# One of eight pairs of h rows by seven block products, with the work around it moved

## The chip, the cores and the metric

The kernel runs on one core of a Trainium2 chip. A core has a matrix engine (TensorE, PE in the profile), two elementwise engines (VectorE, DVE; ScalarE, ACT), a general one (GpSimd, POOL, idle here) and queues that issue DMA (SyncE, SP). Each engine works through its own list of instructions; where one needs another's result it waits on a semaphore. The metric is the device time of one execution in microseconds (us), as the median of several runs.

## The reference

Four batches of 6080 tokens with 256 channels. A channel attention gives, for each batch, a 256 x 256 matrix a, and then each token goes through a feed-forward layer with a squared relu:

```python
qn = q / (np.linalg.norm(q, axis=1, keepdims=True) + 1e-06)
kn = k / (np.linalg.norm(k, axis=1, keepdims=True) + 1e-06)
s = kn.transpose(0, 2, 1) @ qn / tau
s = s - s.max(-1, keepdims=True)
a = np.exp(s)
a /= a.sum(-1, keepdims=True) + 1e-09
x = (v @ a).reshape(B * S, D)
h = np.maximum(x @ w_in, 0.0)
out = h * h @ w_out
```

x has 24320 rows of 256, h 2048 columns. The inputs are float32 except w_in and w_out, which come as float64 and are decoded in the kernel.

## The kernel before

**What is multiplied.** v @ a @ w_in is computed as v @ W, with W = a @ w_in made once per batch (256 x 2048). Each float32 operand is split into a rounded part (hi, written by ScalarE) and the rest (lo, written by VectorE as original minus hi), and each product is three matmuls: hi by hi, hi by lo, lo by hi.

**Blocks and steps.** The tokens of a batch make 12 blocks n: ten of 512 columns and two of 480. A block has 16 steps f, one for each 128 rows of h; two steps are a pair r = f // 2, and part = f % 2. The list `steps` (lines 739 to 743) has four batches of 12 blocks of 16 steps; the first two blocks are interleaved, as W of the first batch is only being made. The loop from line 794 issues, for step i, in this order:

- `first_product` (574): six matmuls of 512 columns into one PSUM tile of the pool `ps_h` (three buffers), then a ScalarE relu into half of the pair's tile x (two buffers);
- one piece of other work (`beside`): the chunks of q and k of the next batch, its softmax and its W (`attention`, 370, and `softmax_and_W`, 402), left out at f = 2 and 3. A chunk takes four steps: at its first a ScalarE cast and a VectorE subtraction, at its third a ScalarE square and a VectorE addition, at its third and fourth six matmuls each. Work at odd steps comes at the step's end;
- at an even step, `parts_of_sums` (611) of the pair before: hi (ScalarE, 1024 columns) and lo (VectorE) of the four sums;
- at an odd step, `squares_and_sums` (598) of this pair: a ScalarE square of 1024 columns, three VectorE sums (of 512, 256 and 256 columns), hi and lo of three of the squares (768 columns);
- at an odd step, one piece of `combine` (680) of the block before, at f = 5, 7 and 9;
- `second_product` (624) of the pair two pairs back (LAG = 2).

**The second product by seven.** For 45 of the 48 blocks the output's 2 x 2 block product takes seven block products, not eight (`seven_products`, 645). Its operands are the pair's squares (slots 0 to 2), their sums (slots 3 to 6), blocks of w_out and sums of them (S1n, S2, S3, S4). `SEVEN` (640) says which of the seven are issued in the even step (three) and in the odd one (four). They accumulate over the block's eight pairs in two PSUM tiles of the pool `ps_acc` (two buffers), one for each part; with the last pair, in the next block's steps 2 and 3, ScalarE copies them out (line 676). The next block's first pair takes the same two tiles at its steps 4 and 5.

**v's parts.** `load_v` brings v of a block (one buffer), `split_v_hi` and `split_v_lo` make hi (ScalarE) and lo (VectorE) of it in the block before, at f = 6 and 8 (line 831).

**Order.** ScalarE, VectorE and TensorE are wrapped in `InProgramOrder` (19): each engine's list has the order in which the Python code issues the instructions. Tiles that share a tag share its buffers; an instruction that writes a buffer waits for the last readers.

Of the kernel before, what the change touches and what calls it, by code (L numbers as in the profile page):

```python
# [30 lines left out]
def kernel(  # L31
# [25 lines left out]
    P = 128  # L57
# [5 lines left out]
    GRP = 512  # L63
    NG = F // GRP
    FPG = GRP // P
    J = 2
    NPAIR = NF // 2
    PPG = FPG // 2
# [162 lines left out]


    W = {}
    now = {"part": 0}
    HEAD = 5
    QK_BUFS = 2
    FAST_TAGS = ("qk",) * QK_BUFS + ("w_lo",) * NG + ("w_hi",) * NG

    class Gram:
# [66 lines left out]
    def start_first(b=0):  # L306

        g = grams[0] = Gram(0)
        total = g.n + HEAD
        AHEAD = len(FAST_TAGS) - 1  # L310

        room = pool.tile([P, HEAD - 1, 2, J, C], F32, tag="wS_lo", name="qk_heads", bufs=1)

        def load(c):
            if c == g.n:
                grams[1] = Gram(1)
            if c < g.n:
                g.load(c, FAST_TAGS[c % len(FAST_TAGS)])
            elif c < total and B > 1:
                grams[1].load(c - g.n, raw=room[:, c - g.n] if c - g.n < HEAD - 1 else None)  # L320

        for c in range(AHEAD):
            load(c)
        for c in range(g.n):
            if c < g.n - LAST:
                for _ in g.products(c, [(g.raws[c], g.raws[c])]):
                    pass
            g.squares(c)
            if c:
                g.add_squares(c - 1)  # L330
            load(c + AHEAD)
            if c in (2, 15):
                weights.load(int(c > 2))
            if c in (13, 14, 15, 17):
                weights.stage(0)
            if c == 19:
                load_v(*order[0])
        for c in range(g.n + AHEAD, total):
            load(c)
        g.add_squares(g.n - 1)  # L340

        def rest():
            for c in range(g.n - LAST, g.n):
                for _ in g.products(c, [(g.raws[c], g.raws[c])]):
                    pass
            yield

        return rest()
# [53 lines left out]
    def softmax_and_W(b):  # L402
# [74 lines left out]
        eT_hi = pool.tile([P, NC, C], F32R, tag="eT_hi", name=f"eT_hi{b}", bufs=1)  # L477
        eT_lo = pool.tile([P, NC, C], F32R, tag="eT_lo", name=f"eT_lo{b}", bufs=1)
# [5 lines left out]
        for g in range(NG):  # L484
            while (b, g) not in may_write_W:
                yield
            if b == 0:
                while g not in wi_first:
                    yield
                hi, lo = wi_first.pop(g)  # L490
                keep_w_in(g, (hi, lo))
            else:
                hi, lo = wi.pop(g)
            w_hi = wpool.tile([P, NC, GRP], F32R, tag="w_hi", name=f"w_hi{b}_{g}")
            w_lo = wpool.tile([P, NC, GRP], F32R, tag="w_lo", name=f"w_lo{b}_{g}")
# [27 lines left out]

            if b == 0:
                for h, terms in ((0, (0, 1)), (1, (0,)), (0, (2,)), (1, (1, 2))):
                    products(h, terms)
                yield
                for h in range(NC):
                    evict(h)
            else:  # L530
                for h in range(NC):
                    products(h)
                    if h == NC - 1 and g + 1 < NG:
                        wi[g + 1] = reload_w_in(b, g + 1)
                    yield
                    evict(h)
                    yield
            W[b, g] = w_hi, w_lo
            yield

# [16 lines left out]
    def once(f, *args):  # L557
        f(*args)
        yield

    def split_v_lo(b, n):
        tn = blocks[n][1]
        raw, hi, _ = V[b, n]
        V[b, n][2] = pool.tile([P, NC, T], F32R, tag="v_lo", name=f"v_lo{b}_{n}")
        vector.tensor_sub(V[b, n][2][:, :, :tn], raw[:, :, :tn], hi[:, :, :tn].bitcast(F32))

    def by_seven(b, n):

# [2 lines left out]
    X = {}  # L571
    G = {}

    def first_product(b, n, f):
        tn = blocks[n][1]
        _, v_hi, v_lo = V[b, n]
        w_hi, w_lo = W[b, f // FPG]
# [20 lines left out]
    def squares_and_sums(b, n, r):  # L598

        x = X[b, n, r]  # L600
        G[b, n, r] = hi, lo = parts_of(b, n, r)
        scalar.activation(x[:, 0:4, :], x[:, 0:4, :], AF.Square)
# [27 lines left out]
    def weights_of(r):  # L630
# [49 lines left out]
    def combine(b, n):  # L680
# [5 lines left out]
        vector.tensor_add(o[:, 1:3, :], o[:, 1:3, :], both(0))  # L686
        yield
        vector.tensor_add(o[:, 4, :], o[:, 4, :], o[:, 2, :])
        vector.tensor_add(o[:, 0, :], o[:, 4, :], o[:, 3, :])
        yield  # L690
        vector.tensor_add(o[:, 3, :], o[:, 3, :], o[:, 2, :])
        vector.tensor_add(o[:, 5:7, :], o[:, 5:7, :], o[:, 3:5, :])
        at = b * N + t0
        out = outT[:, at : at + tn].rearrange("(m p) t -> p m t", p=P)
        for m, k, slot in ((0, 0, 5), (0, 1, 1), (1, 0, 0), (1, 1, 6)):
            nc.sync.dma_start(out[:, m, k * half : (k + 1) * half], o[:, slot, :])
        yield

# [94 lines left out]
    beside = attention_of_others()  # L793
    for i in range(len(steps) + 2 * LAG):
        part = now["part"] = i % 2
        if i < len(steps):
            b, n, f = steps[i]
            at = b * NB + n
# [24 lines left out]
        if part == 1 and i // 2 < len(pairs):  # L823
            squares_and_sums(*pairs[i // 2])
        if part and late_work:
            if next(late_work[0], "end") == "end":
                late_work.pop(0)
        if i >= 2 * LAG:
            second_product(*pairs[i // 2 - LAG], part)
        if i < len(steps):  # L830
            at_hi, at_lo = (None, None) if at == 0 else (12, 13) if at == 1 else (6, 8)
            if i == 2 and len(order) > 2:
                load_v(*order[2])
            if f == at_hi and at + 1 < len(order):
                split_v_hi(*order[at + 1])
            if f == at_lo and at + 1 < len(order):
                split_v_lo(*order[at + 1])
                if at + 2 < len(order):
                    load_v(*order[at + 2])
        if i >= PAIR and part:  # L840
            for gen in gens:
                next(gen, None)
# [27 lines left out]
```

## Time and profile before

| | |
|---|---|
| median of 3 runs | 2220.44 us (2219.77 to 2220.57) |
| the profiled execution | 2222.8 us, of which the span from first to last instruction 2221.0 us |
| mean granted TensorE clock | 0.999 |
| matmul instructions | 13740 |
| matmuls of h (ps_h from v and w) | 3 groups of 1536, of 512 or 480 columns |
| matmuls with sums of w_out (ps_o with wS) | 3 groups of 1440, of 256 or 240 columns |

Busy times are those of an engine, its share is of the span. A group is named by output and inputs: `ps_h<-v_hi,w_hi` are matmuls that write a tile ps_h from v_hi and w_hi. All instructions show line 27, that of the wrapper, so groups are told apart by their tiles: `x<-ps_h` is the relu, `x<-x` on ScalarE the square, `x<-x` on VectorE the three sums, `g_hi<-x` the hi parts (768 columns at odd steps, 1024 at even ones), `g_lo` the lo parts, `o<-ps_o` the copy out of PSUM. A row of the timeline gives start, duration, engine, line, operation, tiles and shape, a count when several are merged, and in brackets how long the engine was idle before and for whom. The end of a matmul is modelled; the start of the next one is what counts for the pace. A row of the waits gives total us, times and the longest. A row of the windows gives the stretch, its length, busy us and instructions of PE, PEld, DVE, ACT and POOL, the granted clock, and DMA.

### The profile page before, as it was taken

How to read it: one execution, taken by the hardware profiler on the slowest of the kernel's cores; microseconds unless marked ns; L12 is line 12 of the kernel's file. 1: busy time of each engine (PE TensorE's matmuls, PEld its weight loads, DVE VectorE, ACT ScalarE, POOL GpSimd, SP SyncE). 2: the span in 40 equal slices, each digit the busy share in tenths (PEclk: the TensorE clock that was granted, in tenths of full speed). 3: DMA queues.
4: the chain of work that ended last, by engine and by line, in shares of the span. 5: the costliest groups of instructions: out<-in, count | busy, mean ns of one | idle time of the engine just before them, and what ended most of it. 6: DMA issues, size and time to landing. Idle time of an engine off the chain costs nothing.

```text
span 2221.0 us, 34359 instructions
## 1 busy us (share of the span) xinstructions
PE 2207.5 (99%) x13740; PEld 1981.4 (89%) x13740; DVE 1761.4 (79%) x2470; ACT 1844.6 (83%) x2294; POOL 0.7 (0%) x6
## 2 busy tenths in 40 slices
PE   8999999999999999999999999999999999999999
PEld 7788999989989999988998999999899888888898
DVE  6878888878778888878777888887877777787773
ACT  5788888888778888888878888888887888888885
POOL 0000000000000000000000000000000000000000
PEclk9999999999999999999999999999999999999999
DMA  9511222100211112110111122110102010010000
GB/s 334 184 67 39 69 66 67 46 29 26 70 66 58 60 60 72 62 41 22 36 68 56 60 66 75 58 53 22 33 25 76 21 36 20 22 37 20 22 26 18
DMA packets 76495, 126.99 MB, mean 57 GB/s; under 512 B 7728, under 2 KB 35120, under 8 KB 76336
## 3 DMA queue, kind: packets, MB, share of 16 engines
q1 hardware_dynamic: 76336, 124.81, 17.2%
q8 instruction: 107, 1.75, 0.3%
q14 instruction: 52, 0.43, 0.1%
HBM read 95.68 MB, written 29.10 MB: 56 GB/s over the span
## 4 chain that ended last, share of the span: by engine, by line
PE 94%; DVE 3%; ACT 1%; DMA 1%; issue 0%; SPq 0%; DVEq 0%; ACTq 0%
PE ps_h L27 46%; PE ps_o L27 41%; PE gram L27 5%; PE ps_w L27 2%; DVE g_lo L27 1%; DMA qk<-in_k 1%; DVE x L27 1%; DVE acc L27 0%; ACT x L27 0%; DMA qk<-in_q 0%; ACT g_hi L27 0%; DVE o L27 0%; PE ps_n L27 0%; ACT sq L27 0%; ACT s L27 0%
## 5 line engine op out<-in xcount | busy, mean ns | idle before, releaser
L27 DVE TENSOR_TENSOR g_lo<-x,g_hi 128x768 fp32r<-128x768 f32 (+2 forms) x744 | 804.4, 1081 | 95.2 <-ACT g_hi L27 94.5
L27 DVE TENSOR_TENSOR x<-x 128x256 f32<-128x256 f32 (+3 forms) x1080 | 551.2, 510 | 279.6 <-ACT x L27 254.7
L27 ACT CAST g_hi<-x 128x768 fp32r<-128x768 f32 (+2 forms) x744 | 697.7, 938 | 24.6 <-DVE x L27 12.0
L27 ACT ACTIVATE x<-ps_h 128x512 f32<-128x512 f32 (+1 forms) x768 | 456.1, 594 | 293.3 <-PE ps_h L27 267.7
L27 PE MATMUL ps_h<-v_hi,w_hi 128*128 128x512 f32 (+1 forms) x1536 | 478.9, 393 | 0.0
L27 PE MATMUL ps_h<-v_hi,w_lo 128*128 128x512 f32 (+1 forms) x1536 | 477.9, 392 | 0.0
L27 PE MATMUL ps_h<-v_lo,w_hi 128*128 128x512 f32 (+1 forms) x1536 | 474.9, 390 | 0.0
L27 ACT ACTIVATE x<-x 128x1024 f32<-128x1024 f32 (+1 forms) x384 | 404.5, 1053 | 11.9
L27 PE MATMUL ps_o<-g_lo,wS_hi 128*128 128x256 f32 (+1 forms) x1440 | 402.5, 279 | 1.3 <-DVE g_lo L27 1.1
L27 PE MATMUL ps_o<-g_hi,wS_lo 128*128 128x256 f32 (+1 forms) x1440 | 401.7, 279 | 0.0
L27 PE MATMUL ps_o<-g_hi,wS_hi 128*128 128x256 f32 (+1 forms) x1440 | 400.8, 278 | 0.0
L27 PEld LDWEIGHTS ps_h<-v_lo,w_hi 128*128 128x128 f32 x1536 | 288.1, 188 | 64.8
L27 PEld LDWEIGHTS ps_h<-v_hi,w_lo 128*128 128x128 f32 x1536 | 288.7, 188 | 61.8
L27 PE MATMUL ps_o<-g_hi,wo_hi 128*128 128x256 f32 (+3 forms) x1176 | 330.9, 288 | 0.9 <-ACT g_hi L27 0.9
L27 PE MATMUL ps_o<-g_hi,wo_lo 128*128 128x256 f32 (+3 forms) x1176 | 331.1, 288 | 0.0
L27 PE MATMUL ps_o<-g_lo,wo_hi 128*128 128x256 f32 (+3 forms) x1176 | 330.6, 288 | 0.1
L27 PEld LDWEIGHTS ps_o<-g_lo,wS_hi 128*128 128x128 f32 x1440 | 271.2, 188 | 18.0 <-DVE g_lo L27 2.3
L27 PEld LDWEIGHTS ps_o<-g_hi,wS_hi 128*128 128x128 f32 x1440 | 270.6, 188 | 15.4
L27 PEld LDWEIGHTS ps_o<-g_hi,wS_lo 128*128 128x128 f32 x1440 | 270.9, 188 | 0.0
L27 PEld LDWEIGHTS ps_h<-v_hi,w_hi 128*128 128x128 f32 x1536 | 239.1, 188 | 5.2
L27 PEld LDWEIGHTS ps_o<-g_hi,wo_hi 128*128 128x128 f32 x1176 | 221.7, 189 | 17.5 <-ACT g_hi L27 1.3
L27 PEld LDWEIGHTS ps_o<-g_lo,wo_hi 128*128 128x128 f32 x1176 | 221.0, 188 | 16.7 <-DVE g_lo L27 0.5
(87 smaller groups left out, 1671.4 us busy)
## 6 DMA issues: line engine op xcount, KB each, us to landing
qk<-in_k SPq DMA_DIRECT2D x87, 256.0 KB, 2.8
qk<-in_q SPq DMA_DIRECT2D x87, 256.0 KB, 3.0
v<-in_vT SPq DMA_DIRECT2D x40, 512.0 KB, 3.8
out_T<-o SPq DMA_DIRECT2D x152, 128.0 KB, 1.7
wi_hi<-wi_kept SPq DMA_DIRECT2D x12, 512.0 KB, 3.2
wi_lo<-wi_kept SPq DMA_DIRECT2D x12, 512.0 KB, 4.1
w_raw<-in_w_in SPq DMA_DIRECT2D x4, 1024.0 KB, 6.0
w_raw<-in_w_out SPq DMA_DIRECT2D x4, 1024.0 KB, 5.5
```

The lines of the kernel that those rows point to most:

```text
L27: return lambda *args, **kwargs: self.tc.keep_in_program_order(issue(*args, **kwargs))
```

## The change

It has five parts.

1. In blocks n >= 3 of the first batch and n >= 1 of the others (42 blocks), the pair r = 5 (f = 10 and 11) takes seven block products for its h. At f = 10 four of them, 12 matmuls of 256 columns into two ps_h tiles; then a chain: ScalarE copies two of them out, VectorE adds one sum (U2), adds it to both halves of the second tile in PSUM, and makes one of the four results. At f = 11 the other three products, 9 matmuls, accumulate onto what stands in PSUM, and three ScalarE relus follow.
2. For that, sums of W's blocks are made once per batch (`sums_of_W`), and sums of v's blocks once per block: `sums_of_v` at the end of f = 0 (three VectorE operations, a ScalarE cast), `sums_of_v_lo` at f = 3 (one VectorE operation).
3. At f = 10 no work goes beside, and the sums of the preceding pair, r = 4, that stood at f = 9, are issued behind the chain; at f = 11 the second product is issued ahead of the first.
4. In the second product the four products of sums are all in the odd step; `combine` uses the new slots.
5. v's hi and lo parts move from f = 6 and 8 to f = 9 and 12, v's load to f = 0. Tiles of w_in, e and one chunk of q and k share other tags.

```diff
     def wi_tiles(b, g):
-        hi = pool.tile([P, NC, GRP], F32R, tag="wi_hi", name=f"wi_hi{b}_{g}", bufs=1)
-        lo = pool.tile([P, NC, GRP], F32R, tag="wi_lo", name=f"wi_lo{b}_{g}", bufs=1)
-        return hi, lo
+        return [
+            pool.tile([P, NC, GRP], F32R, tag="qk", name=f"{name}{b}_{g}", bufs=QK_BUFS) for name in ("wi_hi", "wi_lo")
+        ]
...
+    def sums_of_W(b, r):
+        while now["dec"]:
+            yield
...
+        vector.tensor_add(w, hi, lo)
+        vector.tensor_add(S1, A21, A22)
+        vector.tensor_sub(S3, A11, A21)
+        vector.tensor_sub(S2, S1, A11)
+        vector.tensor_sub(S4, A12, S2)
...
+        scalar.copy(WS[b, r][0], S)
+        vector.tensor_sub(WS[b, r][1], S, WS[b, r][0].bitcast(F32))
...
+    def sums_of_v(b, n):
...
+        vector.tensor_sub(S[:, 0:3:2, :], raw[:, :, half:tn], raw[:, 0, :tn].rearrange("p (k t) -> p k t", k=2))
+        vector.tensor_sub(S[:, 1, :], B22, S[:, 0, :])
+        vector.tensor_sub(S[:, 3, :], B21, S[:, 1, :])
+        scalar.copy(VS[b, n][0], S)
+        now["dec"] = True
+
+    def sums_of_v_lo(b, n):
+        hi, lo, S = VS[b, n]
+        vector.tensor_sub(lo, S, hi.bitcast(F32))
...
+    def seven_first_products(b, n, r, part):
...
+        if part == 0:
...
+            product(one[:, 0], "A11", "B11", start=True)
+            product(one[:, 1], "S2", "T2", stop=True)
+            product(two[:, 0], "S1", "T1", start=True)
+            product(two[:, 1], "S3", "T3")
+            P1, P5, U2 = (x[:, i, :] for i in (4, 5, 6))
+            scalar.copy(P1, one[:, 0])
+            scalar.copy(P5, two[:, 0])
+            vector.tensor_add(U2, one[:, 1], P1)
+            vector.tensor_add(two, two, x[:, 6:7, :].broadcast_to([P, 2, half]))
+            vector.tensor_add(x[:, 3, :], two[:, 1], P5)
+        else:
...
+            product(one[:, 0], "A12", "B21", stop=True)
+            product(two[:, 0], "S4", "B22")
+            product(two[:, 1], "A22", "T4", stop=True)
+            scalar.activation(x[:, 3, :], x[:, 3, :], AF.Relu)
+            scalar.activation(x[:, 0, :], one[:, 0], AF.Relu)
+            scalar.activation(x[:, 1:3, :], two, AF.Relu)
...
     SEVEN = (
-        (None, ("A11", 0), ("A12", 2), ("S2", 5)),
-        (("S1n", 3), ("S3", 4), ("S4", 1), ("A22", 6)),
+        (None, ("A11", 0), ("A12", 2), ("S4", 1)),
+        (("S2", 5), ("S1n", 3), ("S3", 4), ("A22", 6)),
     )
...
         part = now["part"] = i % 2
+        chained, chain_next = (j < len(steps) and first_by_seven(*steps[j]) for j in (i, i + 1))
+        if chained and part:
+            second_product(*pairs[i // 2 - LAG], part)
...
-        if i >= PAIR and steps[min(i, len(steps) - 1)][2] in (2 * LAG - 2, 2 * LAG - 1):
+        if i >= PAIR and (chained and part == 0 or steps[min(i, len(steps) - 1)][2] in (2 * LAG - 2, 2 * LAG - 1)):
             gens = ()
...
+        if chained and part == 0:
+            sums_and_parts(*pairs[i // 2 - 1])
         if part == 0 and 0 <= i // 2 - 1 < len(pairs):
             parts_of_sums(*pairs[i // 2 - 1])
...
-            squares_and_sums(*pairs[i // 2])
+            squares(*pairs[i // 2])
+            if not chain_next:
+                sums_and_parts(*pairs[i // 2])
...
-        if i >= 2 * LAG:
+        if i >= 2 * LAG and not (chained and part):
             second_product(*pairs[i // 2 - LAG], part)
         if i < len(steps):
-            at_hi, at_lo = (None, None) if at == 0 else (12, 13) if at == 1 else (6, 8)
+            at_hi, at_lo = (None, None) if at == 0 else (12, 13) if at == 1 else (9, 12)
...
+            if at > FIRST - 1:
+                if f == 0 and has_sums(b, n):
+                    sums_of_v(b, n)
+                if f == 0 and at + 1 < len(order):
+                    load_v(*order[at + 1])
+                if f == 3 and has_sums(b, n):
+                    sums_of_v_lo(b, n)
```

`squares` and `sums_and_parts` are the two halves of `squares_and_sums`.

More of the change, by code (lines that the diff above doesn't have):

```diff
@@ L65 @@
     FPG = GRP // P
+    QK_BUFS = 2
     J = 2
@@ L233 @@
     W = {}
-    now = {"part": 0}
+    now = {"part": 0, "dec": False}
     HEAD = 5
-    QK_BUFS = 2
     FAST_TAGS = ("qk",) * QK_BUFS + ("w_lo",) * NG + ("w_hi",) * NG
@@ L319, in load @@
             elif c < total and B > 1:
-                grams[1].load(c - g.n, raw=room[:, c - g.n] if c - g.n < HEAD - 1 else None)
+                last = pool.tile([P, 2, J, C], F32, tag="vS_lo", name="qk_head", bufs=1) if c == total - 1 else None
+                grams[1].load(c - g.n, raw=room[:, c - g.n] if last is None else last)
         for c in range(AHEAD):
@@ L476, in softmax_and_W @@
         yield from pause(b, 2, 1)
[L477 to L478 removed]
+        eT = pool.tile([P, 2, NC, C], F32R, tag="qk_hi" if b else "vS_hi", name=f"eT{b}", bufs=1)
+        eT_hi, eT_lo = eT[:, 0], eT[:, 1]
         ps_tv = ps_t.rearrange("p (d c) -> p d c", d=NC)
@@ L572, with first_by_seven, has_sums, product @@
     G = {}
+    H = {}
+    def first_by_seven(b, n, f):
+        return has_sums(b, n) and f // 2 in SEVEN_FIRST
+    def has_sums(b, n):
+        return n >= (1 if b else FIRST)
+    def seven_first_products(b, n, r, part):
+        half = blocks[n][1] // 2
+        _, v_hi, v_lo = V[b, n]
+        def product(ps, a, b_, start=False, stop=False):
+            A, B_ = W_of[a], v_of[b_]
+            for i, (wt, vt) in enumerate(((A[0], B_[0]), (A[0], B_[1]), (A[1], B_[0]))):
+                tensor.matmul(ps, wt, vt, start=start and i == 0, stop=stop and i == 2, skip_group_check=True)
+        A = blocks_of_W(b, r)
+        W_of = {f"A{i + 1}{j + 1}": [a[i][j] for a in A] for i in range(2) for j in range(2)}
+        W_of.update({f"S{i + 1}": [p[:, i, :] for p in WS[b, r]] for i in range(4)})
+        v_of = {
+            f"B{j + 1}{k + 1}": [v[:, j, k * half : (k + 1) * half] for v in (v_hi, v_lo)] for j in range(2) for k in range(2)
+        }
+        v_of.update({f"T{i + 1}": [p[:, i, :] for p in VS[b, n][:2]] for i in range(4)})
+        if part == 0:
+            x = X[b, n, r] = pool.tile([P, 8, half], F32, tag="x", name=f"x{b}_{n}_{r}")
+            one, two = H[b, n, r] = [
+                ps_h.tile([P, 2, T // 2], F32, tag="h", name=f"ps_h{b}_{n}_{r}_{i}")[:, :, :half] for i in range(2)
+            ]
+            product(one[:, 0], "A11", "B11", start=True)
[9 more added lines that the diff above has]
+        else:
+            one, two = H.pop((b, n, r))
+            x = X[b, n, r]
+            product(one[:, 0], "A12", "B21", stop=True)
[4 more added lines that the diff above has]
+            scalar.activation(x[:, 1:3, :], two, AF.Relu)
@@ L837 @@
                 split_v_lo(*order[at + 1])
-                if at + 2 < len(order):
+                if at == 1 and at + 2 < len(order):
                     load_v(*order[at + 2])
+            if at > FIRST - 1:
[5 more added lines that the diff above has]
+                    sums_of_v_lo(b, n)
+            if i in (26, 28):
+                next(first, None)
         if i >= PAIR and part:
```

48 lines of the change are left out of this document (37 added, 11 removed).

## The prediction

> **What bounds the kernel now.** I read the page first, then the waits, then the timeline of one block engine by engine.
>
> ```profile
> span 2221.0 us, 34359 instructions
> PE 2207.5 (99%) x13740; PEld 1981.4 (89%) x13740; DVE 1761.4 (79%) x2470; ACT 1844.6 (83%) x2294; POOL 0.7 (0%) x6
> PE 94%; DVE 3%; ACT 1%; DMA 1%; issue 0%; SPq 0%; DVEq 0%; ACTq 0%
> ```
>
> The chain that ended last is TensorE for 94%. The waits say the same: ScalarE waits for TensorE, VectorE for ScalarE, and TensorE for almost nobody.
>
> ```profile
> ACT x L27 <- PE ps_h L27: 267.7, 465, 4.2
> DVE x L27 <- ACT x L27: 254.7, 276, 2.6
> PE ps_o L27 <- DVE g_lo L27: 1.1, 2, 0.7
> ```
>
> So the time is the number of matmul columns, as long as the other two engines keep their distance. How large that distance is, is read from one block without q and k work beside it (times of TensorE, from the timeline):
>
> ```profile
> 1930.13:1971.99 41.86, 41.86 (x266) 37.60 (x265) 32.26 (x47) 35.31 (x43) 0.00 (x0) 1.00 0.09 26
> 1973.20 0.63 PE L27 MATMUL ps_h<-v_hi,w_hi 128*128 128x512 f32 x2
> ...
> 1974.59 0.28 PE L27 MATMUL ps_o<-g_hi,wo_hi 128*128 128x256 f32 x1
> ...
> 1975.64 0.62 PE L27 MATMUL ps_h<-v_hi,w_hi 128*128 128x512 f32 x2
> ...
> 1977.03 0.28 PE L27 MATMUL ps_o<-g_hi,wS_hi 128*128 128x256 f32 x1
> ...
> 1978.43 0.63 PE L27 MATMUL ps_h<-v_hi,w_hi 128*128 128x512 f32 x2
> ```
>
> A block is 41.86 us and TensorE is busy in all of it. These are its steps f = 4 and 5: six 512-column products of h take 1.39 us (1973.20 to 1974.59), nine 256-column products of the output 1.05 us, twelve of them 1.40 us (1977.03 to 1978.43). Half the columns take half the time, each with its own weight load. The part of ScalarE from f = 0 to f = 4, with the last pair (7) of the block before in flight:
>
> ```profile
> 1964.32 0.60 ACT L27 ACTIVATE x<-ps_h 128x512 f32<-128x512 f32 x1 [0.23 <-PE ps_h L27]
> 1964.90 1.05 ACT L27 CAST g_hi<-x 128x1024 fp32r<-128x1024 f32 x1
> 1966.76 0.60 ACT L27 ACTIVATE x<-ps_h 128x512 f32<-128x512 f32 x1 [0.81 <-PE ps_h L27]
> 1967.39 1.06 ACT L27 ACTIVATE x<-x 128x1024 f32<-128x1024 f32 x1
> 1968.49 0.83 ACT L27 CAST g_hi<-x 128x768 fp32r<-128x768 f32 x1
> 1969.56 0.60 ACT L27 ACTIVATE x<-ps_h 128x512 f32<-128x512 f32 x1 [0.23 <-PE ps_h L27]
> 1970.13 1.05 ACT L27 CAST g_hi<-x 128x1024 fp32r<-128x1024 f32 x1
> 1971.09 0.79 ACT L27 COPY o<-ps_o 128x768 f32<-128x768 f32 x1
> 1972.00 0.60 ACT L27 ACTIVATE x<-ps_h 128x512 f32<-128x512 f32 x1
> 1972.63 1.06 ACT L27 ACTIVATE x<-x 128x1024 f32<-128x1024 f32 x1
> 1973.72 0.83 ACT L27 CAST g_hi<-x 128x768 fp32r<-128x768 f32 x1
> 1974.46 1.01 ACT L27 COPY o<-ps_o 128x1024 f32<-128x1024 f32 x1
> 1975.37 0.60 ACT L27 ACTIVATE x<-ps_h 128x512 f32<-128x512 f32 x1
> ```
>
> Two things are to be seen. The two copies of the old block's sums out of PSUM stand at f = 2 and f = 3, and the new block's products take the same PSUM at f = 4 and f = 5. The second copy ends at 1974.46 + 1.01 = 1975.47 and TensorE wants that PSUM at 1977.03: **1.56 us of slack**. And between the relu of f = 1 (1966.76) and that copy ScalarE idles 0.23 us only: what makes that relu late arrives at the copy almost whole. VectorE in the same stretch:
>
> ```profile
> 1963.26 1.61 DVE L27 TENSOR_TENSOR x<-x 128x512 f32<-128x512 f32 x3 [1.28 <-ACT x L27]
> 1964.78 0.95 DVE L27 TENSOR_TENSOR g_lo<-x,g_hi 128x768 fp32r<-128x768 f32 x1
> 1965.98 1.23 DVE L27 TENSOR_TENSOR g_lo<-x,g_hi 128x1024 fp32r<-128x1024 f32 x1 [0.25 <-ACT g_hi L27]
> ```
>
> Rules of thumb from these rows: an instruction starts 0.03 to 0.04 us after the one it needs; one that needs nothing new starts 0.1 us before the end of its predecessor.
>
> **The change part by part.** *Gain.* A pair's h now costs 2 x 1.39 = 2.78 us; by seven it is 12 + 9 products of 256 columns, 1.40 + 1.05 = 2.45 us. That saves 0.33 us in each of 42 blocks (9 of the first batch, 11 of the three others), 13.9 us; eight of them have 480 columns, so 13.7. The nine added weight loads are in it, since the narrow rows have one load each.
>
> *v's sums at f = 0.* Three VectorE operations of 512, 256 and 256 columns, the sizes of the group that took 1.61 us, and behind them a ScalarE cast of 1024 columns (1.05 us). Both engines keep the order of the program. VectorE has the wide g_lo of pair 7 ahead of them, which waits for ScalarE's wide cast: it ends at 1965.98 + 1.23 = 1967.21, the sums run from 1967.12 to 1968.73, the cast from 1968.77. Queued behind that cast on ScalarE is the relu of f = 1, which then starts at 1969.72 in place of 1966.76: **2.96 us late**, 2 us of it idling. On from there: square 1970.35 to 1971.41, VectorE's sums of pair 0 until 1973.05, so that the wide cast of f = 2 starts at 1973.09, first copy 1974.05, relu 1974.96, square, cast 1976.68, second copy 1977.42 to 1978.43. TensorE stood ready at 1977.03: it waits **1.4 us**, in a block in which all else is as before.
>
> *The chain at f = 10.* Time zero is TensorE's start of that step. The relu of f = 9 is at -1.20, the square at -0.57, v's cast (now at f = 9) at 0.39 to 1.43. The two copies of 256 columns out of PSUM aren't in the trace; the copies out of ps_o of 512 and 768 columns give 0.37.
>
> ```profile
> L27 ACT COPY o<-ps_o 128x512 f32<-128x512 f32 x4 | 2.1, 581 | 0.0
> L27 ACT COPY o<-ps_o 128x768 f32<-128x768 f32 x38 | 30.2, 795 | 0.0
> L27 DVE TENSOR_TENSOR x<-x 128x256 f32<-128x256 f32 x608 | 258.4, 425 | 20.9
> L27 DVE TENSOR_TENSOR x<-x 128x512 f32<-128x512 f32 x304 | 210.2, 691 | 199.0 <-ACT x L27 198.8
> L27 DVE TENSOR_TENSOR v_lo<-v,v_hi 128x1024 fp32r<-128x1024 f32 x40 | 48.8, 1219 | 0.0
> ```
>
> They run at 1.34 and 1.62, VectorE's three additions until 3.33. No row shows an addition that writes PSUM: I take 0.69 us, the row of its size, with the 0.43 of 256 columns and twice the 0.69, 1.4, as ends. TensorE needs the result after 12 + 9 + 12 + 3 products, at 4.20: covered by 0.87 us, so the chain itself stalls nothing. But the preceding pair's sums follow it (3.25 to 4.85) and ScalarE idles until 4.89 for its wide cast, ahead of three relus and the next square. The relu of f = 12 comes at 8.91 where TensorE had it ready at 6.49: 2.4 us late. Pairs recover up to 1.24 us each (5.24 us on TensorE, 4.0 on ScalarE), but v_lo, moved to f = 12, holds VectorE 1.14 us: late by 1.8, 1.5, 1.6 and, at f = 0, still 1.2 us. With that ahead, the relu of f = 1 is 4.5 us late, the first PSUM copy ends at 29.10 (wanted at 27.30), the second at 32.69 (wanted at 29.74): TensorE waits 1.8 and 1.2 us, **3.0 us a block**. Afterwards ScalarE catches up by f = 9, so each block pays it again.
>
> *Blocks with q and k beside them.* f = 10 takes no such work now, so a block takes 3 chunks, not 3.5, and 67 chunks fill some 22 of the 42 blocks. A chunk adds two ScalarE and two VectorE operations of 1024 columns and 1.40 us of TensorE; the same walk gives 2.0 or 2.7 us by where the chunks fall, mean 2.35.
>
> *What costs nothing.* The new order of the output's seven products needs the sums one step later: it gives them 2.45 us more, no time by itself. VectorE's second half of v's sums at f = 3 stands in VectorE's idle time. Sums of W: about 3.1 us of VectorE a batch, in blocks without v's sums, hidden by VectorE's idle 9.6 us there; uncovered, at most 12 us in all. On SP's queue v's load moves to f = 0 behind VectorE's sums, with nothing due behind it until the outputs at f = 9, and is needed 22 us later. w_in's tiles share two buffers with q and k, whose last readers are done first.
>
> ```profile
> v<-in_vT SPq DMA_DIRECT2D x40, 512.0 KB, 3.8
> ```
>
> *Sum.* 20 x 3.0 + 22 x 2.35 = 111.7 us of waits. Against the profiled execution, 2222.8 us: 2222.8 - 13.7 + 111.7 = 2320.8; it stood 2.4 us above the median of the runs, so the **forecast is 2318 us**.
>
> **The rivals.** *Hidden, 2207 us.* One mechanism puts it on the faster side: v's sums need only v, loaded long before, so if VectorE ran them ahead of pair 7's g_lo, ScalarE's cast would not idle and would cost its own 0.95 us; the point that decides is whether the relu of f = 1 is less than 1.56 + 0.23 us late. Then 2220.4 - 13.7. For it: nothing in the data ties them together. Against it: in all rows both engines run in the written order.
>
> *Only the clean wait, 2266 us.* If ScalarE and VectorE recover from the chain before f = 0, 42 x 1.4 = 59 us are lost and 13.7 won. For it: the recovery of 1.24 us a pair; against it: v_lo at f = 12.
>
> *The clock drops, about 2389 us.* The trace has one place where TensorE waited and then worked thinly:
>
> ```profile
> 45.00:50.00 5.00, 3.21 (x17) 2.76 (x17) 4.55 (x15) 0.29 (x1) 0.00 (x0) 0.93 1.05 392
> 50.00:55.00 5.00, 5.00 (x17) 3.43 (x17) 2.72 (x10) 1.52 (x3) 0.00 (x0) 0.73 0.74 244
> ```
>
> With 3.21 of 5 us busy the granted clock fell to 0.93 and then 0.73 of full, which lost 5 x 0.07 + 5 x 0.27 = 1.7 us. If each block's two waits did the same, 42 x 1.7 = 71 us come on top. Against it: the two waits have 2.45 us of dense products between them. The Trainium skill, TensorE: Matmul & The Clock Gate, section "HAM oscillation — how this bites in real kernels", asks for idle gaps above some 3.4 us before the clock drops; by that rule nothing is added here, and the sum stays. Its section "A second HAM failure mode: psum-queue depth-cycling" says that frequent short idles between groups of matmuls are enough; by that one this rival comes true. The rows just shown lean to the second, since no idle there reached 3.4 us.
>
> **How the numbers follow.** Forecast, 2.0 to 3.2 us a block, 2285 to 2340: 0.47. Clean wait, 2245 to 2285: 0.15. Part hidden, 2216 to 2245: 0.06. Hidden: 0.20. Clock: 0.12. The dear end of the PSUM addition, 0.7 us a block, would make it 2347. Leaving out the clock's case, the range is 2205 to 2345. A measurement of this kernel can tell 0.2%, about 4.4 us. Faster by more: 0.20; within: 0.03; slower: 0.77.
>
> **What would show it.** In the changed profile, the waits should have TensorE's ps_o behind ScalarE's o, over 80 us in all; ScalarE's cast of v's sums should idle 2 to 3 us behind VectorE at each f = 0, with the relu after it 3 to 5 us behind its product; the addition into PSUM should be near 0.69 us and TensorE's second half of the seven products should wait for none. If ps_o does not wait for o, the forecast is wrong at the slack of 1.56 us; if it waits 1.4 us a block, only the residue of the chain is. If TensorE waits at f = 11 for VectorE, the 0.87 us was.

## The result, and the profile after

The changed kernel takes **2325.22 us** (2325.01 to 2328.94, 4 runs) against 2220.3 us before on the same chip: a ratio of 1.0475, with a 95% interval of 1.0463 to 1.0488. It is slower by 105 us. The page of the changed kernel, with its span, the engines and the chain that ended last:

```profile
span 2323.2 us, 35621 instructions
PE 2221.4 (96%) x14118; PEld 1985.4 (85%) x14118; DVE 1925.8 (83%) x2788; ACT 1873.7 (81%) x2466; POOL 0.7 (0%) x6
DVE 38%; PE 29%; ACT 27%; issue 5%; DMA 1%; SPq 0%; DVEq 0%; ACTq 0%
```

TensorE's 94% of the chain have become 29%. The chain now runs round the three engines, although TensorE is still busy 96% of the span and VectorE and ScalarE only 83 and 81%: they wait for one another. The waits of the changed kernel (engine, what it waits for, total us, times, longest) say where:

```profile
ACT g_hi L27 <- DVE x L27: 155.6, 171, 3.5
ACT vS_hi L27 <- DVE v_sums L27: 130.9, 42, 3.7
...
ACT x L27 <- PE ps_h L27: 87.8, 131, 4.2
PE ps_o L27 <- ACT o L27: 75.0, 76, 2.8
...
PE ps_h L27 <- DVE x L27: 0.7, 1, 0.7
```

ScalarE waited 267.7 us for TensorE before, and 87.8 now. In exchange it waits 42 times for VectorE's sums of v, 3.1 us each, and TensorE waits for ScalarE's copies out of PSUM. The last row is TensorE's wait for the result of the new chain: once. One block without q and k beside it, from f = 0 to f = 5, first VectorE's timeline, then ScalarE's, then TensorE's:

```profile
2055.96 1.22 DVE L27 TENSOR_TENSOR g_lo<-x,g_hi 128x1024 fp32r<-128x1024 f32 x1 [0.25 <-ACT g_hi L27]
2057.10 0.68 DVE L27 TENSOR_TENSOR v_sums<-v 128x512 f32<-128x512 f32 x1
2057.82 0.89 DVE L27 TENSOR_TENSOR v_sums<-v,v_sums 128x256 f32<-128x256 f32 x2
```

```profile
2054.88 1.05 ACT L27 CAST g_hi<-x 128x1024 fp32r<-128x1024 f32 x1 [0.31 <-DVE x L27]
2058.74 1.05 ACT L27 CAST vS_hi<-v_sums 128x1024 fp32r<-128x1024 f32 x1 [2.81 <-DVE v_sums L27]
2059.70 0.59 ACT L27 ACTIVATE x<-ps_h 128x512 f32<-128x512 f32 x1
...
2064.01 0.79 ACT L27 COPY o<-ps_o 128x768 f32<-128x768 f32 x1
...
2067.17 1.00 ACT L27 COPY o<-ps_o 128x1024 f32<-128x1024 f32 x1
```

```profile
2062.51 0.63 PE L27 MATMUL ps_h<-v_hi,w_lo 128*128 128x512 f32 x2
2064.85 0.38 PE L27 MATMUL ps_o<-g_hi,wo_hi 128*128 128x256 f32 x1 [1.71 <-ACT o L27]
2065.08 0.28 PE L27 MATMUL ps_o<-g_lo,wo_hi 128*128 128x256 f32 x1
2065.19 0.28 PE L27 MATMUL ps_o<-g_hi,wo_lo 128*128 128x256 f32 x1
...
2066.01 0.62 PE L27 MATMUL ps_h<-v_hi,w_hi 128*128 128x512 f32 x2
...
2068.23 0.39 PE L27 MATMUL ps_o<-g_hi,wS_hi 128*128 128x256 f32 x1 [0.68 <-ACT o L27]
```

VectorE does pair 7's wide g_lo first, then v's sums; ScalarE's cast stands idle 2.81 us for them, with the relu of f = 1 queued behind it. The first copy then ends at 2064.80 and TensorE, which could have started that product at 2062.97, starts at 2064.85: 1.88 us later. At f = 5 it could have gone on at 2066.01 + 1.39 = 2067.40 and starts at 2068.23, 0.83 us later.

Block lengths below are the distances between successive first copies (`COPY o<-ps_o 128x768`) on ScalarE. Without q and k beside, a block took 41.87 us before and 44.50 us now; with q and k 46.95 (mean of two that alternate) and 48.51. To compare kernels I also count **TensorE's waits**: of all pairs of successive matmuls after the first 66 us, the time from start to start beyond the pace (0.2345 us for 512 columns, 0.1185 for 256, in proportion for 480 and 240; products of one column are left out), where it is over 0.06 us. Before that was 7.9 us in all, 4.7 of it at products of ps_o; now it is 122.1 us, 100.9 of it at products of ps_o. The largest of the others is 2.5 us, near a batch's end.

### The profile page after: what moved, and what is told of

It reads as the page before. It is cut to its first block, busy times and chain, and to the rows that moved or that the text cites. A ratio compares the mean times of both kernels' runs of the same rounds, so it can differ in the third digit from the quotient of the medians.

```text
span 2323.2 us, 35621 instructions
## 1 busy us (share of the span) xinstructions
PE 2221.4 (96%) x14118; PEld 1985.4 (85%) x14118; DVE 1925.8 (83%) x2788; ACT 1873.7 (81%) x2466; POOL 0.7 (0%) x6
## 3 DMA queue, kind: packets, MB, share of 16 engines
HBM read 95.68 MB, written 29.10 MB: 54 GB/s over the span
## 4 chain that ended last, share of the span: by engine, by line
DVE 38%; PE 29%; ACT 27%; issue 5%; DMA 1%; SPq 0%; DVEq 0%; ACTq 0%
DVE x L27 16%; ACT x L27 14%; PE ps_h L27 13%; PE ps_o L27 12%; DVE g_lo L27 10%; ACT g_hi L27 6%; DVE acc L27 3%; ACT o L27 3%; DVE v_sums L27 3%; DVE v_lo L27 2%; ACT vS_hi L27 2%; PE ps_w L27 2%; DVE qk_lo L27 2%; PE gram L27 2%; DVE ps_h L27 1%
## 5 line engine op out<-in xcount | busy, mean ns | idle before, releaser
L27 ACT CAST g_hi<-x 128x768 fp32r<-128x768 f32 (+2 forms) x744 | 697.7, 938 | 166.7 <-DVE x L27 155.6
L27 ACT ACTIVATE x<-ps_h 128x512 f32<-128x512 f32 (+2 forms) x768 | 440.5, 579 | 80.2 <-PE ps_h L27 78.4
L27 PE MATMUL ps_h<-v_hi,w_hi 128*128 128x512 f32 (+3 forms) x1452 | 450.0, 386 | 8.8 <-ACT x L27 8.8
L27 PE MATMUL ps_h<-v_hi,w_lo 128*128 128x512 f32 (+3 forms) x1452 | 448.5, 385 | 0.0
L27 PE MATMUL ps_h<-v_lo,w_hi 128*128 128x512 f32 (+3 forms) x1452 | 446.5, 384 | 0.0
L27 ACT ACTIVATE x<-x 128x1024 f32<-128x1024 f32 (+3 forms) x426 | 421.5, 989 | 12.2 <-DVE x L27 0.3
L27 PE MATMUL ps_o<-g_hi,wS_hi 128*128 128x256 f32 (+1 forms) x1440 | 405.7, 282 | 26.6 <-ACT o L27 26.6
L27 PE MATMUL ps_o<-g_hi,wo_hi 128*128 128x256 f32 (+3 forms) x1176 | 336.3, 292 | 49.5 <-ACT o L27 48.4
L27 PEld LDWEIGHTS ps_h<-v_lo,w_hi 128*128 128x128 f32 x1452 | 272.3, 188 | 57.7
L27 PEld LDWEIGHTS ps_h<-v_hi,w_lo 128*128 128x128 f32 x1452 | 272.8, 188 | 55.2
L27 PEld LDWEIGHTS ps_o<-g_lo,wS_hi 128*128 128x128 f32 x1440 | 271.6, 189 | 12.2
L27 PEld LDWEIGHTS ps_h<-v_hi,w_hi 128*128 128x128 f32 x1452 | 228.3, 188 | 14.8 <-ACT x L27 10.2
```

What stands on the lines that cost most here:

```text
L27: return lambda *args, **kwargs: self.tc.keep_in_program_order(issue(*args, **kwargs))
```

## The experiments

Each edit is of the changed kernel, unless another is named. Ratios are to the kernel before.

**The cast of v's sums later.** It leaves f = 0 for f = 4, behind the copies, and the lo part goes to f = 6.

```diff
-        scalar.copy(VS[b, n][0], S)
...
+    def cast_sums_of_v(b, n):
+        scalar.copy(VS[b, n][0], VS[b, n][2])
...
-                if f == 3 and has_sums(b, n):
+                if f == 4 and has_sums(b, n):
+                    cast_sums_of_v(b, n)
+                if f == 6 and has_sums(b, n):
                     sums_of_v_lo(b, n)
```

> Only ScalarE's cast of v's sums moves, from f = 0 to f = 4, behind both copies of the old block's PSUM; VectorE's second half moves from f = 3 to f = 6; the amount of work is the same. Theory (the cast, standing behind VectorE on ScalarE's list, makes the relu of f = 1 late and with it the two PSUM copies): TensorE's waits of ps_o for o fall from 75 us to under 10 us and the time to about 2216 us (2208 to 2224), a little above 2207, since the sums of W showed 13.0 us of ScalarE waiting. Rival 'load' (ScalarE and VectorE simply have too much to do in each block): 2300 us or more. Rival 'chain' (the chain at f = 10 with the sums behind it is what is late): 2265 to 2300 us.

Measured: 2279.88 us, ratio 1.0268 [1.0253, 1.0284]. A miss by 64 us: only 45 of the 105 us went. The waits of this kernel:

```profile
ACT g_hi L27 <- DVE x L27: 242.9, 207, 3.5
...
PE ps_h L27 <- DVE x L27: 19.5, 35, 1.1
...
PE ps_o L27 <- ACT o L27: 4.9, 12, 0.7
```

TensorE's wait for the copies is gone (75.0 to 4.9), as it should be, and another has grown: ScalarE's wide cast waits for VectorE's sums of a pair, 242.9 us against 155.6. In a block without q and k (42.75 us long) ScalarE never waits for TensorE; it idles for more than 0.32 us at four places, each time behind VectorE, at f = 8, 10, 14 and 2:

```profile
1998.35 1.05 ACT L27 CAST g_hi<-x 128x1024 fp32r<-128x1024 f32 x1 [1.26 <-DVE x L27]
...
2005.47 1.05 ACT L27 CAST g_hi<-x 128x1024 fp32r<-128x1024 f32 x1 [2.27 <-DVE x L27]
...
2015.37 1.05 ACT L27 CAST g_hi<-x 128x1024 fp32r<-128x1024 f32 x1 [1.00 <-DVE x L27]
...
2025.08 1.06 ACT L27 CAST g_hi<-x 128x1024 fp32r<-128x1024 f32 x1 [1.38 <-DVE x L27]
```

The four have in common that VectorE had something else ahead of a pair's sums: the lo part of v's sums, the chain, v's lo part, v's sums. TensorE's waits come to 74.9 us, 25.1 of them at f = 11, in 37 blocks, behind a chain that is now late. So the cast was one such place among several, and with it gone the next bound is 45 us away, not 109.

**VectorE's sums ahead of pair 7's wide g_lo.** The three operations (`sums_of_v`, now without the cast) are issued right behind the h products of f = 0 and their relu; the cast, again as `cast_sums_of_v`, stays where it was. This is the mechanism of the prediction's rival "hidden".

```diff
             first_product(b, n, f)
+            if at > FIRST - 1 and f == 0 and has_sums(b, n):
+                sums_of_v(b, n)
...
                 if f == 0 and has_sums(b, n):
-                    sums_of_v(b, n)
+                    cast_sums_of_v(b, n)
```

> Only VectorE's three operations on v at f = 0 move ahead of pair 7's wide g_lo; ScalarE's cast stays at the end of f = 0. Theory, walked through: VectorE has the sums at 21.5 instead of 23.0 us behind the start of f = 10, so the relu of f = 1 is about 3.0 us late instead of 4.5, and TensorE's wait in a block falls by about 1.4 us: 2325 - 42 x 1.4 = 2266 us (2250 to 2285). Rival 'load': 2310 us or more. Rival 'any wait of ScalarE for VectorE is harmless, it is the cast's own length': no change, 2320 us or more.

Measured: 2250.06 us, ratio 1.0135 [1.012, 1.015], at the cheap end of what was expected. The order of two VectorE pieces alone is worth 75 us. But it hides nothing fully:

```profile
ACT vS_hi L27 <- DVE v_sums L27: 51.7, 41, 1.9
```

**No chain.** The pair r = 5 takes its 12 wide products again; v's and W's sums are still made, and nothing reads them.

```diff
-        return has_sums(b, n) and f // 2 in SEVEN_FIRST
+        return False
```

> All pairs take 12 wide products again, so no chain, no products by seven for h and no sums deferred; v's sums and W's sums are still made (and not used), v's parts stay at f = 9 and 12. Theory: the gain of 13.7 us is gone, the clean wait of 1.4 us a block stays, with W's sums on top: 2220 + 59 + 9 = 2288 us (2272 to 2300). Rival 'chain': the wait goes with the chain, 2220 to 2240 us. Rival 'load': about 2300 us, little changed.

Measured: 2278.56 us, ratio 1.0262 [1.0247, 1.0277]. This is the cost of v's and W's sums, the cast and the moved work with neither gain nor chain: 58.2 us over the kernel before, 1.39 us in each of 42 blocks. A block without q and k is 43.20 us long, 1.33 more than before.

**v's sums once.** Only the first block makes them; the others read its tiles.

```diff
+                if f == 0 and has_sums(b, n) and at == FIRST:
+                    sums_of_v(b, n)
                 if f == 0 and has_sums(b, n):
-                    sums_of_v(b, n)
+                    VS[b, n] = VS[order[FIRST]]
...
-                if f == 3 and has_sums(b, n):
+                if f == 3 and has_sums(b, n) and at == FIRST:
                     sums_of_v_lo(b, n)
```

> v's sums are made for the first such block alone and used in all of them, so h is wrong in one pair of eight in the others; the chain, the products by seven and W's sums stay. Theory: the chain is covered, nothing waits for v's sums: 2214 us (2206 to 2222). Rival 'chain': 2265 us or more. Rival 'load': 2240 us or more, as VectorE keeps the chain's 1.5 us and only 2.8 us a block go.

Measured: 2222.62 us, ratio 1.0009 [0.9999, 1.0018], a little above its range. Chain, W's sums and the moved parts stay, and TensorE's waits fall from 122.1 to 20.2 us. What the chain leaves behind it costs almost nothing as long as v's sums, their cast and their lo part do not follow in the same block. Taking all three out gives back 103 us; moving the cast alone gave back 45.

**Pair 4's sums ahead of the chain.** They go back to f = 9; `sums_of_pair` are VectorE's three operations, the parts stay at f = 10.

```diff
-            sums_and_parts(*pairs[i // 2 - 1])
+            parts_of_pair(*pairs[i // 2 - 1])
...
-            if not chain_next:
+            if chain_next:
+                sums_of_pair(*pairs[i // 2])
+            else:
                 sums_and_parts(*pairs[i // 2])
```

> Only the three VectorE sums of pair 4 go back to f = 9, ahead of the chain; their hi and lo parts stay behind it. Theory (ScalarE's 2.25 us of idling behind the chain leave a residue that adds to the lateness at f = 0): about 1.4 us a block less waiting, as in the kernel without the chain, 2325 - 59 = 2266 us (2250 to 2282), and the chain, some 0.4 us later, still inside TensorE's cover. Rival 'the chain has no slack to give': TensorE waits at f = 11 for VectorE's additions, 2300 us or more. Rival 'only the cast at f = 0 counts': 2315 us or more.

Measured: 2312.82 us, ratio 1.0415 [1.04, 1.0431]: a miss; the rival holds that the chain has no slack to give. VectorE's timeline at f = 9 and 10 of this kernel, and TensorE's waits:

```profile
2028.04 1.15 DVE L27 TENSOR_TENSOR o<-o 128x256 f32<-128x256 f32 x2
2029.11 0.42 DVE L27 TENSOR_TENSOR x<-ps_h,x 128x256 f32<-128x256 f32 x1
```

```profile
PE ps_o L27 <- ACT o L27: 36.4, 58, 2.7
PE ps_h L27 <- DVE x L27: 31.4, 56, 1.4
```

The wait for the copies halves (75.0 to 36.4), and TensorE now waits for the chain. Not the sums alone make it late: combine's third piece, 1.15 us, comes between them and the chain's first addition.

**Everything in pieces.** On top of the last: v's sums at f = 1 and 3, their cast at f = 4, their lo part in halves at f = 6 and 8, v's lo part in halves at f = 12 and 13, W's sums in four pieces; v's load goes to f = 4.

```diff
-                if f == 0 and has_sums(b, n):
-                    sums_of_v(b, n)
...
+                if f in (1, 3) and has_sums(b, n):
+                    sums_of_v(b, n, f // 2)
+                if f == 4 and has_sums(b, n):
+                    cast_sums_of_v(b, n)
...
-                if f == 3 and has_sums(b, n):
-                    sums_of_v_lo(b, n)
+                if f in (6, 8) and has_sums(b, n):
+                    sums_of_v_lo(b, n, f == 8)
```

> All of it at once: pair 4's sums ahead of the chain; v's sums in two pieces at f = 1 and 3, their cast at f = 4, the second half in two pieces at f = 6 and 8; v's lo in two pieces at f = 12 and 13; W's sums of the later batches in four pieces. Same work. Theory (each engine waits for the other through extra VectorE work standing in one lump ahead of a pair's sums; pieces of 0.6 us fit in VectorE's idle time of each pair): 2212 us (2205 to 2225), faster than before. Rival 'the two engines are bound by their sum of work whatever its place': 2240 us or more.

Measured: 2250.66 us, ratio 1.0136 [1.0119, 1.0153]. A miss by 39 us, most of it at one place: TensorE's waits behind the copies are gone altogether, but 29 us stand at f = 11, in 38 blocks, behind the chain. So the next edit takes combine's third piece away from it, from f = 9 to 11:

```diff
-        if part and late_work:
+        if part and late_work and not chain_next:
```

> The spread kernel with the third piece of combine moved from f = 9 to f = 11, so that nothing but pair 4's sums stands ahead of the chain on VectorE. In the spread kernel nearly all that was left of TensorE's waiting was 0.7 to 0.9 us a block at f = 11. Theory (VectorE's 1.1 us of combine ahead of the chain, against TensorE's cover of 0.87 us): that wait goes, 2250.7 - 36 = 2214 us (2207 to 2222), faster than before. Rival 'the chain is late whatever stands ahead of it': 2240 us or more.

Measured: **2218.59 us** (2216.84 to 2219.46, 11 runs), ratio 0.999 [0.9981, 0.9999], within its range. Its waits:

```profile
ACT g_hi L27 <- DVE x L27: 67.1, 136, 1.4
...
PE ps_h L27 <- DVE vS_lo L27: 5.6, 5, 1.6
...
PE ps_h L27 <- DVE x L27: 1.6, 3, 0.7
```

The same arithmetic as in the changed kernel, in another order, takes 107 us less. A block without q and k takes 41.58 us here, 0.29 less than before. TensorE's waits come to 16.1 us, 6.7 of them for the lo part of v's sums (the expectation that follows has 14.3 and 6.6). With its halves one step earlier, at f = 5 and 7:

> The version with everything in pieces (2218.6 us) with the two halves of v's sums' lo parts issued one step earlier, at f = 5 and 7. What was left of waits there is 14.3 us, 6.6 of it products that wait for vS_lo at seven places. If those come from the halves' place alone, the time falls by up to 6.6 us: 2212.5, range 2208 to 2217. Rival: the halves then stand ahead of a piece of combine or of a pair's three sums, and the wait moves to another tile: 2218 or more.

Measured: 2218.35 us, ratio 0.9989 [0.998, 0.9998]. A miss, and the rival holds: waits for vS_lo fall from 6.7 to 1.3 us, those at f = 11 rise from 1.9 to 5.8, and the sum is 16.3.

**The pieces, with the sums behind the chain.** The version in pieces, with pair 4's sums put back behind the chain as the change has them.

```diff
-            parts_of_pair(*pairs[i // 2 - 1])
+            sums_and_parts(*pairs[i // 2 - 1])
...
-            if chain_next:
-                sums_of_pair(*pairs[i // 2])
-            else:
+            if not chain_next:
                 sums_and_parts(*pairs[i // 2])
```

> The same, but pair 4's sums behind the chain as in the changed kernel. Theory: the chain has its whole cover, ScalarE idles some 2 us behind it, and with v's sums in pieces it has made that up before the copies of f = 2 and 3: 2216 us (2207 to 2230). Rival 'the order of sums and chain decides': 2240 us or more, with waits of ps_o for o.

Measured: 2253.86 us, ratio 1.0149 [1.0135, 1.0163], a miss by 38 us. ScalarE's wait behind VectorE's sums rises from 67.1 to this, and TensorE waits 53 us in all, 21 of them at q and k's products:

```profile
ACT g_hi L27 <- DVE x L27: 157.0, 185, 2.3
```

So even where the copies are never late, sums put behind the chain cost 35 us.

**v's parts back.** The changed kernel with v's parts at f = 6 and 8, where they were.

```diff
-            at_hi, at_lo = ... else (12, 13) if at == 1 else (9, 12)
+            at_hi, at_lo = ... else (12, 13) if at == 1 else (6, 8)
```

> The changed kernel with v's hi and lo parts back at f = 6 and 8. Theory (v's lo part at f = 12 costs 0.67 us of the recovery between the chain and f = 0): 0.6 us a block less, 2325 - 26 = 2299 us (2288 to 2312). Rival (what is taken from behind the chain is put ahead of it): no change or a later chain, 2318 us or more.

Measured: 2349.23 us, ratio 1.0579 [1.0565, 1.0594]: a miss with the wrong sign. VectorE's and ScalarE's timeline at f = 8 to 10:

```profile
2058.76 1.22 DVE L27 TENSOR_TENSOR v_lo<-v,v_hi 128x1024 fp32r<-128x1024 f32 x1
...
2059.89 1.15 DVE L27 TENSOR_TENSOR o<-o 128x256 f32<-128x256 f32 x2
...
2060.96 0.42 DVE L27 TENSOR_TENSOR x<-ps_h,x 128x256 f32<-128x256 f32 x1
...
2064.20 1.05 ACT L27 CAST g_hi<-x 128x1024 fp32r<-128x1024 f32 x1 [3.33 <-DVE x L27]
```

v's lo part and combine's third piece stand one behind the other ahead of the chain, whose first addition is then late; TensorE waits 28 us at f = 11, and ScalarE's wide cast idles 3.33 us, not 2.25. The prediction held the move to f = 12 for a cost. Against f = 6 and 8 it saves 24 us here.

**W's sums in pieces.** The changed kernel with W's sums in four pieces.

> Only W's sums of the three later batches are cut in four pieces, each a step apart. Theory (ScalarE's wait of 3.3 us for them, in each of three batches, makes TensorE wait 2 to 4 us a batch beside the waits in the blocks): 2325 - 9 = 2316 us (2312 to 2320). Rival (those waits are made up before the next copy out of PSUM): 2323 us or more.

Measured: 2326.4 us, ratio 1.0477 [1.0461, 1.0492]. A miss: nothing is won. TensorE's waits for ScalarE's x at products of h do fall, from 8.8 to 3.8 us, and those for the copies rise from 75.0 to 78.3. By the count above TensorE waits 124.1 us in all, against 122.1.

**v's sums and their cast back at f = 0, chain harmless.** The version in pieces (2218.6 us) with v's sums whole at f = 0, the cast behind them, the lo part at f = 3 and v's load at f = 0.

> The same version in pieces, but with v's sums whole at f = 0, their cast right behind them and the lo part at f = 3, as in the changed kernel. That leaves one of the two things that the prediction added up: the clean wait of 1.4 us a block at TensorE's products of the old block's PSUM, without a residue of the chain. By the prediction's terms 2218.6 + 42 x 1.4 = 2277, range 2262 to 2285, with waits of ps_o behind ScalarE's o of 45 to 65 us. Rival: what makes the relu of f = 1 late is mostly the lateness that the chain leaves, so that with it gone the cast costs under 0.7 us a block: below 2248.

Measured: 2303.08 us, ratio 1.037 [1.0356, 1.0384]. A miss by 26 us: this alone takes back 84.5 us, 2.0 a block. It is dearer beside q and k (48.40 us a block against 45.96) than without (43.36 against 41.58). TensorE's timeline without q and k:

```profile
2004.75 0.39 PE L27 MATMUL ps_o<-g_hi,wo_hi 128*128 128x256 f32 x1 [0.56 <-ACT o L27]
...
2008.12 0.39 PE L27 MATMUL ps_o<-g_hi,wS_hi 128*128 128x256 f32 x1 [0.68 <-ACT o L27]
```

And ScalarE's at f = 0 of a block with q and k:

```profile
967.50 1.04 ACT L27 CAST qk_hi<-qk 128x1024 fp32r<-128x1024 f32 x1
968.47 1.05 ACT L27 CAST g_hi<-x 128x1024 fp32r<-128x1024 f32 x1
973.13 1.05 ACT L27 CAST vS_hi<-v_sums 128x1024 fp32r<-128x1024 f32 x1 [3.61 <-DVE v_sums L27]
```

There a chunk's cast of q or k stands at f = 0 ahead of the wide cast, and the cast of v's sums idles 3.61 us, not 2.81. The lengths of such blocks in a row are alike (48.38 to 48.42 us), as the chunks' casts stand at the same steps in each. That the chunk's place makes the difference is read from these rows; it was not tried by moving it. In the changed kernel the chunks fall otherwise: there it is a chunk's square, of the same size, that stands at f = 0, and the cast of v's sums idles 3.43 us:

```profile
926.57 1.05 ACT L27 ACTIVATE qk<-qk 128x1024 f32<-128x1024 f32 x1
...
931.98 1.05 ACT L27 CAST vS_hi<-v_sums 128x1024 fp32r<-128x1024 f32 x1 [3.43 <-DVE v_sums L27]
```

So 48.40 us here and 48.51 in the changed kernel suggest that with q and k beside, v's sums and their cast cost almost as much without a late chain as with it. As the chunks stand at other steps in the two kernels, that is not shown.

## Why the prediction was right

It forecast 2318 us, giving this case a chance of 0.47, and 2325 was measured. Its mechanism is confirmed along the walk through a block without q and k, and most sizes too. That the total came so close is in part luck, as told under what was costed at nothing.

**The gain.** 0.33 us a block was said, 13.7 in all. The version in pieces shows 41.87 - 41.58 = 0.29 us a block, 42 x 0.29 = 12.2 us. The 21 narrow products take a little longer than said: in the changed kernel they start over 1.42 us at f = 10 (2035.70 to 2037.12) and 1.08 at f = 11 (2039.57 to 2040.65), 2.50 us for 2.45.

**v's sums at f = 0.** "Clean", the wait was to be 1.4 us a block, 58.8 us in all. The kernel without the chain lost 58.2, and in its blocks without q and k 1.33 us each. The order of VectorE's pieces decides, as was argued: with the sums ahead of the wide g_lo 75 us come back.

**The chain at f = 10.** TensorE's start of f = 10 is at 2035.70 in this block. VectorE's part, then ScalarE's of the changed kernel:

```profile
2037.43 0.42 DVE L27 TENSOR_TENSOR x<-ps_h,x 128x256 f32<-128x256 f32 x1 [0.92 <-ACT x L27]
2037.96 0.70 DVE L27 TENSOR_TENSOR ps_h<-ps_h,x 128x512 f32<-128x512 f32 x1
2038.69 0.42 DVE L27 TENSOR_TENSOR x<-ps_h,x 128x256 f32<-128x256 f32 x1
2039.04 1.60 DVE L27 TENSOR_TENSOR x<-x 128x512 f32<-128x512 f32 x3
```

```profile
2040.67 1.05 ACT L27 CAST g_hi<-x 128x1024 fp32r<-128x1024 f32 x1 [2.25 <-DVE x L27]
...
2044.66 0.59 ACT L27 ACTIVATE x<-ps_h 128x512 f32<-128x512 f32 x1
...
2050.56 1.05 ACT L27 CAST g_hi<-x 128x1024 fp32r<-128x1024 f32 x1 [0.99 <-DVE x L27]
```

The additions end 3.41 us after that start (3.33 was said) and TensorE wants the result at 4.22 (4.20): the chain is covered, with 0.8 us to spare. The unknown addition into PSUM took 0.70 us, by its own row of the groups:

```profile
L27 DVE TENSOR_TENSOR ps_h<-ps_h,x 128x512 f32<-128x512 f32 x34 | 23.8, 700 | 3.9 <-DVE x L27 0.5
```

The wide cast starts at 4.97 (4.89) and the relu of f = 12 at 8.96 (8.91). On at f = 1, whose product TensorE started at 2053.56 and had ready 1.54 us later, as at f = 12, the relu starts 4.6 us behind it (4.5). The first copy ends at 29.10, the very number of the walk, the second at 32.47 (32.69).

**The waits a block.** Without q and k 3.0 us were said, as 1.8 and 1.2. Measured 1.88 and 0.83, and 44.50 - 41.58 = 2.92 us in the block's length. With q and k 2.35 were said and 48.51 - 45.96 = 2.55 measured. **The term that was off** is the second wait, 1.2 for 0.83; the copy before it ended 0.22 us earlier than walked. The two waits and the late product behind each, 0.1 us, make the 2.92. In all, ps_o was to wait for o over 80 us: the view of the waits has 75.0, the count from start to start 100.9.

**What was left behind by the chain.** The prediction's sum gave this residue 111.7 - 58.8 = 52.9 us. From the measured times it is 2325.2 - 2278.6 + 12.2 = 58.8 us. But this split rests on the kernel without the chain alone. In the version in pieces v's sums and their cast at f = 0 cost 84.5 us, not 58, and in blocks without q and k 1.78 us, not 1.33; why, was not tried. So in those blocks the chain's residue lies at 44.50 - 43.36 = 1.14 us by the one and at 2.92 - 1.33 = 1.59 by the other, where 3.0 - 1.4 = 1.6 was said; beside q and k it may be near nothing (48.51 - 48.40). The prediction walked both costs in one go, and its total does not hang on the split.

**What was costed at nothing.** W's sums are no cost that could be had back: in pieces they gave nothing. TensorE's other waits, outside ps_o, rose by 18.0 us in all (3.2 to 21.2); the prediction had no term for them. It priced the waits of ps_o too high by about as much (111.7 us, where they rose by 96.2), so the total hides an error on each side, and that the two cancel is luck. The move of v's lo part to f = 12 was booked as part of the residue; against leaving it at f = 8 it is a saving.

**The rivals.** "Hidden" is false as its price was put: VectorE's sums ahead gave 2250, not 2207. "Only the clean wait" would have been 2266; the wait is as large as said in the kernel without the chain, but the chain's residue comes on top. "The clock drops" is false as it was priced. A window on the wait at f = 4 and what follows (length, busy us and instructions of PE, PEld, DVE, ACT and POOL, granted clock, DMA):

```profile
2062.00:2067.00 5.00, 3.29 (x19) 2.56 (x19) 3.62 (x6) 4.63 (x7) 0.00 (x0) 1.00 0.02 6
```

TensorE is busy 3.29 of 5 us, as thinly as in the stretch before the change where the clock fell to 0.93, and the clock stays at 1.00. No block's pair of waits loses it. One other stretch of the changed kernel does, where TensorE waits for a tile of the next batch's softmax (a row of the timeline, then a window):

```profile
570.70 0.35 PE L27 MATMUL ps_h<-vS_hi,WS_hi 128*128 128x240 f32 x1 [2.30 <-DVE eT L27]
```

```profile
570.00:575.00 5.00, 4.30 (x24) 4.33 (x25) 3.73 (x8) 1.43 (x3) 0.00 (x0) 0.66 0.16 52
```

That is 5 x 0.34 = 1.7 us, as much as the one stretch of the kernel before, so it adds nothing between the two. The Trainium skill, TensorE: Matmul & The Clock Gate, section "HAM oscillation — how this bites in real kernels", asks for gaps above some 3.4 us before the clock drops. The gaps in the blocks are 1.71 and 0.68 us, and there the trace agrees. In the stretch just shown it does not: the clock fell behind 2.30 us, and it held behind a gap of 2.77 us that ended at 552.47, so here the length of one gap does not decide. The rule in the Trainium skill's section "A second HAM failure mode: psum-queue depth-cycling" of the same page, that frequent short idles suffice, did not come true with two such idles a block. But in the kernel with pair 4's sums ahead of the chain two waits close together, of 0.94 and 0.70 us (to 572.76 and 574.07), were enough: its clock is 0.95 from 570 to 575 us and 0.71 in the next five.

**Where my own story failed** was behind the prediction. I held the cast at f = 0 for the whole loss; moving it away gave back 45 us of 105. What the experiments show in its place: in this kernel a lump of VectorE work ahead of what ScalarE needs next holds up ScalarE, with it the relus queued behind, and so VectorE's own next input. In a block of the changed kernel three such lumps show: ScalarE idles 2.81 us behind v's sums, 2.25 behind the chain and 0.99 behind v's lo part at f = 12 (rows above). The first two are new. The lo part of v's sums makes no such idling at f = 3; moved to f = 6 with the later cast, it did. Taking one lump away uncovers the next; with v's sums and lo parts in pieces and nothing but pair 4's sums ahead of the chain, the loss is gone. What remains open is why the last 8.2 us (16.1 us of waits against 7.9 before) could not be moved; the one try shifted them to another tile.

## What to carry to other kernels

When two engines hand work to and fro in written order, as here, an added operation can cost not its duration but the idling of whoever stands behind it; walk both engines' lists over a whole period before placing it, and place it in pieces where each finds its inputs done. Saving 0.3 us a block on the bounding engine is worth little while the other two are 80% busy: the best order found here wins 0.1%, below what I called measurable, and a bad one loses 5.8%. A removed wait should be expected to uncover the next, so price the second bound as well before promising the whole gain.

## What was not expected of the hardware

The first matmul of 256 columns after a wait has its successor 0.23 us behind it (2064.85 to 2065.08 above), where the pace is 0.12; two waits a block thus cost 0.2 us beyond themselves. VectorE's addition in place on 512 columns in PSUM takes 0.700 us (34 of them), hardly more than the 0.691 us of the same size outside PSUM.
